# Seven products instead of eight from chunk 4 on in a spectral filter with a gated MLP

## The chip, the cores and the metric

The kernel runs on one core of a Trainium2 chip. The metric is the device time of one execution in microseconds (us); the time before is the median of three runs. A separate execution was taken with the hardware profiler; all lines of the profile come from it. Its engines are named PE (TensorE, matmuls), PEld (TensorE's weight loads, which overlap PE), DVE (VectorE), ACT (ScalarE), POOL (GpSimd) and SP (SyncE, whose queue issues all transfers).

## What is computed

Two branches on the same x of 8192 tokens by 448 features, joined at the end. Cut to what matters:

```
xn = layernorm(x)                                  # over the 448 features
s  = irfft2( mlp( rfft2(xn) ) )                    # per frequency: 4 blocks of 112 features,
                                                   # complex 112x112, relu, 112x112, soft shrink
g  = silu( (gelu(x @ w_gate) * (x @ w_up)) @ w_down )   # 448 -> 1792 -> 448
out = x + s * g
```

In the kernel both branches start from the same x in float32. A float32 value is carried as two float16 values, a high and a low part, and a float32 product as three float16 matmuls (high by high, high by low, low by high) accumulated in one PSUM bank.

## The kernel before

**Two streams of work share the engines.** The foreground is the gated MLP (function `ffn`, line 1895, which runs `chunk`, line 1945). The 8192 tokens are 16 chunks of 512; the 1792 inner features are 14 tiles of 128. Pass 0 takes tiles 0 to 7 for chunks 2 to 15 (chunks 0 and 1 are done at the start in another way, `plain`), pass 1 takes tiles 8 to 13 for all 16. The partial result of pass 0 goes to memory (`prt`) and is added in pass 1. The background is the spectral branch in three phases: phase 1 (`chunk1`, line 837) normalises 16 chunks of x, prepares their token factors (`xts` in memory) for the MLP and does the first step of the transform; phase 2 (`group`, line 2268) does the frequencies; phase 3 (`tiles3`, line 2432) does the last step, multiplies by g and stores. Beside phase 1, `weights` (line 2774) prepares the weight tiles.

**Units and the down projection of a chunk.** In both products the 2x2 block product is done with seven instead of eight block products (Strassen-Winograd). In the gate and up projections, `unit` (line 1433) does this throughout: a pair of tiles is a unit of 7 products of 10 or 12 matmuls of 256 columns, four units a chunk in pass 0. In the down projection there are two forms. `down` (line 1866) is the plain one: for each of 4 blocks of 128 tokens and each tile, three matmuls of 448 columns into a bank bd. `down2` (line 1682) does seven products of 224 columns: it needs factors of w_down (sums of its blocks, prepared by `factors2` and stored in memory as `dsp`) and sums of h, the MLP's inner result. The sums are made by `sums` (line 1535) inside each unit, from the tiles gl and u, by additions, casts and subtractions; they are stored in the tiles h and left. The tile gl has one buffer in pass 0; it is taken by the second gelu of a unit and given back when `sums` has read it. The partial results of `down2` meet in four tiles th, first written by ACT, later added to by DVE.

**When the seven products begin.** At the start of a chunk, `chunk` looks at two flags (line 1948). `products` is set by `weights` once the first four factor tiles are stored, plus 3 us (line 2795). If it is set, and the pass is 1 or the chunk's number is at least 9, the flag `seven` is set for good, and `factors_in(0)` (line 1236) is issued 2 us later: 26 transfers from `dsp` into the tiles dw, wt and left, where dw until then held the plain w_down.

**The order of the work.** All instructions are put in order by a planner at build time (`Pace`, line 59). It keeps a modelled time, the modelled end of each engine's work and a modelled cost of each operation; each engine then runs its instructions in the order in which the planner emitted them. Foreground work is emitted when its inputs are due; background work waits until the engine is modelled as free (`clear`, line 99). The table STEPS (line 43) is read by modelled time, and each row holds, after its time: us added to the landing of a transfer; how far an engine may be booked ahead before background waits; a factor on modelled durations of ACT, DVE and POOL; a shift in the choice between DVE and POOL where either can do an operation (`Either`, line 295); and a factor on the spacing of background work. The background's spacing is T1 and DT for phase 1 (line 886: chunk c starts at T1, then each DT later times that factor), END2 for phase 2 and END3 for phase 3 (line 2388: the pieces left are spread over the time left).

Of the kernel before, what the change touches and what calls it, by code (L numbers as in the profile page):

```python
# [22 lines left out]
NG = 16  # L23
# [35 lines left out]
class Pace:  # L59
# [498 lines left out]
def afno_geglu_kernel(ctx, tc, x, gu, raw, wd, mlp, b1, b2, c_m, c_mt, c_small, c_rows, out):  # L558
# [103 lines left out]
    def ev(*key):  # L662
        return EV.setdefault(key, Event())
# [742 lines left out]
    state = {"direct": NG}  # L1406
# [538 lines left out]
    def chunk(p, i):  # L1945
        nf = PF[p][1]
        nxt = (p, i + 1) if i + 1 < NG else ((1, 0) if p == 0 else None)
        if "products" in state and "seven" not in state and (p or i >= 9):
            state["seven"] = True
            pace.spawn(later(lambda: factors_in(0)), pace.now + 2.0)  # L1950
        seven = "seven" in state
        if "h" not in state:
            state["h"] = yield from HT.get()
        h = state["h"]

        def hv(f, s):
# [72 lines left out]
        yield from down(p, i, 1, 0, cut, hv)  # L2029
        yield pe()  # L2030
        for a in (0, 1):
            yield from down(p, i, a, cut, nf, hv)
            yield pe()
        for a in (2, 3):
            yield from down(p, i, a, 0, nf, hv)
            yield pe()
        HT.put(state.pop("h"))

    def later(fn):
        fn()  # L2040
        return
        yield
# [809 lines left out]
```

## Time and profile before

| What | us |
|---|---|
| time before, median of 3 runs | 1727.75 (1726.9 to 1728.06) |
| the profiled execution's own time | 1729.31 |
| its span (first to last instruction) | 1727.2 |
| chunk 2 of pass 0 begins | 142 |
| chunk 4 of pass 0 begins | 259 |
| chunk 9 of pass 0 begins, the first with seven products | 538 |
| last transfer of phase 1's token factors issued | 635 |
| first load of phase 3 issued | 1472 |
| last matmul ends | 1721 |

The times of chunks are the starts of their first matmul of the kind bx<-xta,wt. In the profile, an operation is named out<-in by the program's tiles without buffer numbers, and nearly all of them carry line 290, where the planner records them; so groups are told apart by their tiles and shapes. bx and by are the PSUM banks of the units, bd those shared by the down projection and the background. In a row of the stages, each engine has its busy time and, in brackets, the number of its instructions; then follow the clock granted to TensorE (1.00 is full), the mean busy share of the 16 DMA engines, and GB/s. In a row of the timeline, the start comes first, then how long the run of like instructions lasted to its modelled end, and their number at the end.

### The profile page before, as it was taken

To read this page: it belongs to the slowest core of one execution; us is meant where nothing else is said; L and a number is where in the kernel's file an instruction comes from. 1 tells how busy PE (TensorE), PEld (TensorE's weight loads), DVE (VectorE), ACT (ScalarE), POOL (GpSimd) and SP (SyncE) were. 2 spreads that over 40 slices of the span, in tenths; PEclk is the share of its full clock that TensorE was granted. 3 is DMA by queue.
4 is the path that set the end of the run, shared out by engine and by line. 5 is a ranking of instruction groups with operands and counts; after the bars stand their busy time and mean duration, and the time that the engine had idled before them with its cause. 6 is when DMAs were issued, how large, how long until landed. Compare 5 with 4: busy or idle time off the path is not lost.

```text
span 1727.2 us, 41012 instructions
## 1 busy us (share of the span) xinstructions
PE 1709.1 (99%) x15654; PEld 1435.5 (83%) x15654; DVE 1345.0 (78%) x2317; ACT 1103.3 (64%) x2242; POOL 1014.2 (59%) x1410
## 2 busy tenths in 40 slices
PE   9999999999999999999999999999999999999998
PEld 4447677766777999998999999999999999889886
DVE  8998888778777878778786777787776786577776
ACT  6767766676756657678676667777676665333333
POOL 2487656677735785456374466654555654555556
PEclk9999999999999999999999999999999999999999
DMA  7348986997756753253535875454645544999996
GB/s 275 119 154 256 276 237 207 265 281 202 231 163 189 208 135 77 60 128 88 131 91 172 214 174 122 123 135 109 156 123 137 120 105 123 280 321 314 296 306 229
DMA packets 438308, 316.62 MB, mean 183 GB/s; under 512 B 305792, under 2 KB 409600, under 8 KB 436320
## 3 DMA queue, kind: packets, MB, share of 16 engines
q1 hardware_dynamic: 437824, 313.99, 64.4%
q8 instruction: 122, 2.00, 0.5%
q14 instruction: 74, 0.61, 0.1%
q10 hardware_dynamic: 288, 0.03, 0.0%
HBM read 137.93 MB, written 108.25 MB: 143 GB/s over the span
## 4 chain that ended last, share of the span: by engine, by line
PE 87%; DVE 6%; ACT 2%; DMA 2%; POOL 2%; issue 1%; SPq 0%; POOLq 0%; DVEq 0%; ACTq 0%
PE bd L290 35%; PE bx L290 30%; PE by L290 22%; DMA prt<-th 1%; DVE st L290 1%; ACT wt L290 1%; DVE raws L290 0%; POOL st L290 0%; DVE ysb L290 0%; DVE wt L290 0%; DVE dw L290 0%; DVE left L290 0%; DVE u L290 0%; DMA xta<-xts 0%; DVE h L290 0%
## 5 line engine op out<-in xcount | busy, mean ns | idle before, releaser
L290 PEld LDWEIGHTS <-wt 128*128 128x128 f16 x9142 | 885.4, 98 | 160.2 <-issue 8.2
L290 PE MATMUL bx<-xta,wt 128*128 128x256 f16 (+1 forms) x2819 | 354.0, 275 | 3.5 <-ACT by L290 2.6
L290 PEld LDWEIGHTS <-h 128*128 128x128 f16 x2711 | 259.8, 98 | 75.5 <-POOL h L290 1.6
L290 PE MATMUL by<-xtb,wt 128*128 128x256 f16 x2080 | 255.2, 273 | 0.4 <-DVE by L290 0.3
L290 PE MATMUL bd<-dw,h 128*128 128x448 f16 (+1 forms) x1536 | 243.1, 306 | 1.0 <-DVE ysb L290 0.7
L290 POOL TENSOR_TENSOR wt<-wt 128x256 f32<-128x256 f32 x181 | 140.2, 775 | 94.0 <-DVE wt L290 84.7
L290 PE MATMUL bx<-xtb,wt 128*128 128x256 f16 x1248 | 154.3, 274 | 2.2 <-DVE v L290 2.2
L290 PE MATMUL by<-xta,wt 128*128 128x256 f16 (+1 forms) x899 | 123.8, 282 | 0.1
L290 POOL TENSOR_TENSOR h<-wt,h 128x512 f16<-128x512 f32 (+1 forms) x92 | 96.1, 1058 | 35.9 <-ACT h L290 35.4
L290 DVE TENSOR_TENSOR by<-bx,u 128x512 f32<-128x512 f32 x104 | 72.4, 696 | 52.9 <-PE bx L290 44.9
L290 ACT ACTIVATE u<-by,fc 128x512 f32<-128x512 f32 (+1 forms) x118 | 73.6, 636 | 51.5 <-PE by L290 49.4
L290 PE MATMUL bx<-left,wt 128*128 128x256 f16 x816 | 99.9, 272 | 0.0
L290 DVE TENSOR_TENSOR v<-bx,u 128x512 f32<-128x512 f32 x104 | 71.4, 686 | 36.1 <-PE bx L290 35.5
L290 PE MATMUL bd<-dw,wt 128*128 128x224 f16 (+1 forms) x816 | 97.6, 264 | 0.5 <-DVE left L290 0.5
L290 POOL CAST zs<-t 112x256 f16<-112x256 f32 (+2 forms) x45 | 21.3, 474 | 123.1 <-DVE t L290 107.9
L290 ACT COPY u<-by 128x512 f32<-128x512 f32 x104 | 60.8, 585 | 50.2 <-PE by L290 49.4
L290 ACT CAST h<-wt 128x512 f16<-128x512 f32 (+1 forms) x128 | 68.5, 536 | 31.4 <-DVE wt L290 25.1
L290 PE MATMUL bd<-w2t,wn 113*128 113x112 f16 (+1 forms) x1152 | 77.6, 212 | 0.0
L290 ACT COPY by<-bx 128x512 f32<-128x512 f32 x104 | 59.8, 575 | 21.1 <-PE bx L290 20.8
L290 PE MATMUL bd<-wt,h 128*128 128x224 f16 x603 | 72.0, 259 | 0.8 <-POOL h L290 0.8
L290 PEld LDWEIGHTS <-wn 113*128 113x128 f16 (+1 forms) x1152 | 69.1, 97 | 2.1
L290 DVE SCALAR_TENSOR_TENSOR u<-by,fc,u 128x512 f32<-128x512 f32 (+1 forms) x86 | 55.2, 656 | 18.7 <-PE by L290 12.9
(283 smaller groups left out, 3764.8 us busy)
## 6 DMA issues: line engine op xcount, KB each, us to landing
xts<-sx SPq DMA_DIRECT2D x32, 480.0 KB, 3.6
x<-in_x SPq DMA_DIRECT2D x17, 896.0 KB, 6.2
t<-ysb SPq DMA_DIRECT2D x64, 224.0 KB, 3.8
prt<-th SPq DMA_DIRECT2D x64, 224.0 KB, 3.2
vt<-va SPq DMA_DIRECT2D x256, 56.0 KB, 2.1
left<-prt SPq DMA_DIRECT2D x64, 224.0 KB, 3.7
u<-t SPq DMA_DIRECT2D x32, 448.0 KB, 6.0
x<-in_x SPq DMA_DIRECT2D x32, 448.0 KB, 6.6
```

What stands on the lines that cost most here:

```text
L290: return self.pace.issue(self.name, kind, out, ins, lambda: fn(out, *args, **kw))
```

## The change

Four edits. The first lets the seven products begin at chunk 4 instead of chunk 9 of pass 0. The second sets the first phase's chunks at another start and spacing. The third moves the due time of phase 3, END3. The fourth replaces the table STEPS from end to end; four of its rows are shown. Nothing else of the program differs.

```diff
-STEPS = ((0, 2.75, 0.05, 1.0, 0.0, 1.0), (15, 2.75, 0.05, 1.0, 0.0, 1.0),
+STEPS = ((0, 2.75, 0.05, 1.0, -0.3, 1.0), (15, 2.75, 0.05, 1.0, -0.3, 1.0),
...
-(125, 2.5, 0.15, 1.04, 0.0, 1.0), (150, 2.5, 0.15, 1.04, 0.0, 1.0),
+(125, 2.0, 0.05, 1.07, 0.2, 1.0), (150, 2.0, 0.05, 1.07, 0.2, 1.0),
...
-(375, 3.0, 0.05, 1.03, -0.2, 0.9), (400, 3.0, 0.05, 1.03, -0.2, 0.9),
+(375, 2.0, 0.05, 1.08, 0.0, 1.06), (400, 2.0, 0.05, 1.08, 0.0, 1.06),
...
-(1525, 1.25, 0.05, 1.025, -0.5, 1.0), (1550, 1.25, 0.05, 1.025, -0.5, 1.0),
+(1525, 2.0, 0.05, 0.965, -0.5, 1.16), (1550, 2.0, 0.05, 0.965, -0.5, 1.16),
...
-    T1, DT = 84.0, 34.0
+    T1, DT = 80.0, 32.5
...
-        if "products" in state and "seven" not in state and (p or i >= 9):
+        if "products" in state and "seven" not in state and (p or i >= 4):
...
-    END1, END2, END3 = T1 + NG * DT + 12.0, 1450.0, 1716.0
+    END1, END2, END3 = T1 + NG * DT + 12.0, 1450.0, 1704.0
```

END1 is used nowhere else.

More of the change, by code (lines that the diff above doesn't have):

```diff
@@ L42 @@
 EPS = 1e-5
-STEPS = ((0, 2.75, 0.05, 1.0, 0.0, 1.0), (15, 2.75, 0.05, 1.0, 0.0, 1.0), (25, 2.75, 0.05, 0.96, 0.2, 1.0), (35, 2.75, 0.05, 0.96, 0.2, 1.0), (45, 2.75, 0.05, 1.08, 0.1, 1.0), (55, 2.75, 0.05, 1.08, 0.1, 1.0), (65, 2.75, 0.05, 1.07, 0.0, 1.0), (75, 2.75, 0.05, 1.07, 0.0, 1.0), (87, 2.75, 0.15, 0.98, -0.1, 1.0), (100, 2.75, 0.15, 0.98, -0.1, 1.0), (125, 2.5, 0.15, 1.04, 0.0, 1.0), (150, 2.5, 0.15, 1.04, 0.0, 1.0), (175, 2.5, 0.15, 1.04, 0.2, 1.0), (200, 2.5, 0.15, 1.04, 0.2, 1.0), (225, 3.0, 0.15, 1.08, -0.2, 1.0), (250, 3.0, 0.15, 1.08, -0.2, 1.0), (275, 3.0, 0.15, 1.08, -0.2, 1.0), (300, 3.0, 0.15, 1.08, -0.2, 1.0), (325, 3.0, 0.05, 1.03, -0.2, 1.0), (350, 3.0, 0.05, 1.03, -0.2, 1.0), (375, 3.0, 0.05, 1.03, -0.2, 0.9), (400, 3.0, 0.05, 1.03, -0.2, 0.9), (425, 2.5, 0.15, 1.04, -0.5, 1.06), (450, 2.5, 0.15, 1.04, -0.5, 1.06), (475, 2.5, 0.1, 1.04, 0.0, 1.0), (500, 2.5, 0.1, 1.04, 0.0, 1.0), (525, 2.5, 0.1, 1.04, -0.3, 1.0), (550, 2.5, 0.1, 1.04, -0.3, 1.0), (575, 2.5, 0.1, 1.04, -0.2, 0.94), (600, 2.5, 0.1, 1.04, -0.2, 0.94), (625, 2.5, 0.1, 1.06, -0.2, 0.94), (650, 2.5, 0.1, 1.06, -0.2, 0.94), (675, 2.5, 0.1, 1.03, -0.2, 0.94), (700, 2.5, 0.1, 1.03, -0.2, 0.94), (725, 2.5, 0.1, 1.03, -0.3, 0.94), (750, 2.5, 0.1, 1.03, -0.3, 0.94), (775, 3.0, 0.05, 1.04, -0.5, 1.0), (800, 3.0, 0.05, 1.04, -0.5, 1.0), (825, 2.5, 0.05, 1.02, -0.5, 1.0), (850, 2.5, 0.05, 1.02, -0.5, 1.0), (875, 2.5, 0.05, 1.05, -0.5, 1.0), (900, 2.5, 0.05, 1.05, -0.5, 1.0), (925, 2.5, 0.05, 1.05, -0.5, 0.94), (950, 2.5, 0.05, 1.05, -0.5, 0.94), (975, 2.5, 0.05, 1.05, -0.5, 0.94), (1000, 2.5, 0.05, 1.05, -0.5, 0.94), (1025, 4.0, 0.05, 1.05, -0.5, 0.9), (1050, 4.0, 0.05, 1.05, -0.5, 0.9), (1075, 4.0, 0.05, 1.05, -0.5, 0.75), (1100, 4.0, 0.05, 1.05, -0.5, 0.75), (1125, 2.75, 0.05, 1.04, 0.0, 0.94), (1150, 2.75, 0.05, 1.04, 0.0, 0.94), (1175, 1.75, 0.05, 1.075, 0.0, 1.0), (1200, 1.75, 0.05, 1.075, 0.0, 1.0), (1225, 1.75, 0.05, 1.045, -0.5, 0.94), (1250, 1.75, 0.05, 1.045, -0.5, 0.94), (1275, 1.75, 0.05, 1.055, -0.5, 1.0), (1300, 1.75, 0.05, 1.055, -0.5, 1.0), (1325, 1.25, 0.05, 0.995, -0.5, 1.03), (1350, 1.25, 0.05, 0.995, -0.5, 1.03), (1375, 1.25, 0.05, 0.995, -0.5, 0.93), (1400, 1.25, 0.05, 0.995, -0.5, 0.93), (1425, 1.25, 0.05, 0.995, -0.5, 0.93), (1450, 1.25, 0.05, 0.995, -0.5, 0.93), (1475, 1.25, 0.05, 1.025, -0.5, 1.0), (1500, 1.25, 0.05, 1.025, -0.5, 1.0), (1525, 1.25, 0.05, 1.025, -0.5, 1.0), (1550, 1.25, 0.05, 1.025, -0.5, 1.0), (1575, 1.25, 0.05, 1.055, -0.5, 1.06), (1600, 1.25, 0.05, 1.055, -0.5, 1.06), (1625, 1.25, 0.05, 1.055, -0.5, 1.06), (1650, 1.25, 0.05, 1.055, -0.5, 1.06), (1675, 1.25, 0.1, 1.045, -0.5, 1.06), (1700, 1.25, 0.1, 1.045, -0.5, 1.06), (1725, 2.75, 0.05, 0.94, 0.4, 1.0))
@@ new lines @@
+STEPS = ((0, 2.75, 0.05, 1.0, -0.3, 1.0), (15, 2.75, 0.05, 1.0, -0.3, 1.0), (25, 2.75, 0.05, 0.96, 0.2, 1.0), (35, 2.75, 0.05, 0.96, 0.2, 1.0), (45, 2.75, 0.05, 1.08, 0.3, 1.0), (55, 2.75, 0.05, 1.08, 0.3, 1.0), (65, 2.75, 0.05, 1.07, 0.0, 1.0), (75, 2.75, 0.05, 1.07, 0.0, 1.0), (87, 2.75, 0.05, 1.07, 0.0, 1.0), (100, 2.75, 0.05, 1.07, 0.0, 1.0), (125, 2.0, 0.05, 1.07, 0.2, 1.0), (150, 2.0, 0.05, 1.07, 0.2, 1.0), (175, 2.0, 0.2, 1.07, 0.2, 1.0), (200, 2.0, 0.2, 1.07, 0.2, 1.0), (225, 2.0, 0.05, 1.08, 0.2, 1.06), (250, 2.0, 0.05, 1.08, 0.2, 1.06), (275, 2.0, 0.05, 1.08, -0.1, 1.06), (300, 2.0, 0.05, 1.08, -0.1, 1.06), (325, 2.0, 0.05, 1.08, -0.1, 1.06), (350, 2.0, 0.05, 1.08, -0.1, 1.06), (375, 2.0, 0.05, 1.08, 0.0, 1.06), (400, 2.0, 0.05, 1.08, 0.0, 1.06), (425, 3.0, 0.3, 1.03, -0.2, 0.9), (450, 3.0, 0.3, 1.03, -0.2, 0.9), (475, 2.5, 0.3, 1.04, 0.0, 1.0), (500, 2.5, 0.3, 1.04, 0.0, 1.0), (525, 2.5, 0.3, 1.04, 0.2, 1.0), (550, 2.5, 0.3, 1.04, 0.2, 1.0), (575, 2.5, 0.05, 1.04, 0.0, 1.0), (600, 2.5, 0.05, 1.04, 0.0, 1.0), (625, 2.5, 0.3, 1.04, -0.3, 0.9), (650, 2.5, 0.3, 1.04, -0.3, 0.9), (675, 2.5, 0.05, 1.04, -0.3, 0.9), (700, 2.5, 0.05, 1.04, -0.3, 0.9), (725, 2.5, 0.1, 1.03, -0.4, 1.0), (750, 2.5, 0.1, 1.03, -0.4, 1.0), (775, 3.0, 0.05, 1.08, -0.4, 1.0), (800, 3.0, 0.05, 1.08, -0.4, 1.0), (825, 2.5, 0.05, 1.0, -0.5, 1.0), (850, 2.5, 0.05, 1.0, -0.5, 1.0), (875, 2.5, 0.05, 1.0, -0.5, 1.0), (900, 2.5, 0.05, 1.0, -0.5, 1.0), (925, 2.5, 0.05, 1.05, -0.5, 0.94), (950, 2.5, 0.05, 1.05, -0.5, 0.94), (975, 2.5, 0.05, 1.02, -0.5, 0.94), (1000, 2.5, 0.05, 1.02, -0.5, 0.94), (1025, 3.25, 0.05, 1.02, -0.2, 0.94), (1050, 3.25, 0.05, 1.02, -0.2, 0.94), (1075, 3.25, 0.05, 1.02, -0.5, 0.94), (1100, 3.25, 0.05, 1.02, -0.5, 0.94), (1125, 3.25, 0.05, 1.02, -0.5, 0.94), (1150, 3.25, 0.05, 1.02, -0.5, 0.94), (1175, 3.5, 0.05, 1.02, -0.5, 0.84), (1200, 3.5, 0.05, 1.02, -0.5, 0.84), (1225, 1.75, 0.05, 1.045, -0.5, 0.94), (1250, 1.75, 0.05, 1.045, -0.5, 0.94), (1275, 1.75, 0.05, 1.045, -0.5, 0.94), (1300, 1.75, 0.05, 1.045, -0.5, 0.94), (1325, 2.25, 0.05, 1.045, -0.5, 0.94), (1350, 2.25, 0.05, 1.045, -0.5, 0.94), (1375, 2.25, 0.05, 1.045, -0.5, 0.94), (1400, 2.25, 0.05, 1.045, -0.5, 0.94), (1425, 1.25, 0.05, 0.965, -0.5, 1.0), (1450, 1.25, 0.05, 0.965, -0.5, 1.0), (1475, 1.25, 0.05, 0.965, -0.5, 1.1), (1500, 1.25, 0.05, 0.965, -0.5, 1.1), (1525, 2.0, 0.05, 0.965, -0.5, 1.16), (1550, 2.0, 0.05, 0.965, -0.5, 1.16), (1575, 2.0, 0.05, 0.965, -0.5, 1.16), (1600, 2.0, 0.05, 0.965, -0.5, 1.16), (1625, 2.0, 0.05, 0.965, -0.5, 1.16), (1650, 2.0, 0.05, 0.965, -0.5, 1.16), (1675, 1.25, 0.05, 1.055, -0.4, 1.06), (1700, 1.25, 0.05, 1.055, -0.4, 1.06), (1725, 2.75, 0.05, 0.94, 0.4, 1.0))
```

## Prediction

> **What bounds the kernel now.** I read the page first: busy time by engine and the chain that ended last.
>
> ```profile
> span 1727.2 us, 41012 instructions
> PE 1709.1 (99%) x15654; PEld 1435.5 (83%) x15654; DVE 1345.0 (78%) x2317; ACT 1103.3 (64%) x2242; POOL 1014.2 (59%) x1410
> PE 87%; DVE 6%; ACT 2%; DMA 2%; POOL 2%; issue 1%; SPq 0%; POOLq 0%; DVEq 0%; ACTq 0%
> ```
>
> PE is busy 99% of the span and is 87% of the chain. A busy PE need not be a PE at its rate, so next come the stages (PE's busy time is the second figure), and what PE waited for from 140 to 540 us (us in total, times, longest).
>
> ```profile
> core 0: us, PE busy (x) PEld busy (x) DVE busy (x) ACT busy (x) POOL busy (x), PEclk, DMA share, GB/s
> 150.00:200.00 50.00, 47.40 (x343) 34.01 (x341) 40.88 (x81) 34.85 (x74) 31.30 (x59) 0.97 0.86 244
> 250.00:540.00 290.00, 287.71 (x2169) 211.46 (x2168) 228.55 (x429) 191.88 (x370) 191.26 (x343) 1.00 0.77 224
> 540.00:1000.00 460.00, 458.94 (x4780) 423.90 (x4778) 352.75 (x610) 316.38 (x683) 267.50 (x362) 1.00 0.52 134
> 1000.00:1700.00 700.00, 699.51 (x7032) 638.11 (x7030) 525.19 (x828) 410.50 (x817) 389.40 (x445) 1.00 0.67 186
> ...
> PE bx L290 <- ACT by L290: 2.6, 2, 1.9
> PE bx L290 <- DVE v L290: 1.4, 1, 1.4
> PE bd L290 <- DVE ysb L290: 0.7, 1, 0.7
> PE by L290 <- DVE by L290: 0.3, 1, 0.3
> ```
>
> From 250 us on PE is idle for 2.3 + 1.1 + 0.5 us in 1450. So whatever leaves PE's stream of matmuls leaves the time, as long as the other engines keep up, and whatever they add to PE's waits comes back whole.
>
> **The change, part by part.** *Fewer columns.* In each of chunks 4 to 8 of pass 0 the plain down projection (4 token blocks x 8 row tiles x 3 matmuls of 448 columns = 96) gives way to seven products (7 x 4 pairs x 2 halves x 3 = 168 of 224 columns, and one of 64). Prices come from the start of one run to the start of the next:
>
> ```profile
> 191.92 10.96 PE L290 MATMUL bd<-dw,h 128*128 128x448 f16 x57
> 202.71 0.49 PE L290 MATMUL bx<-xta,wt 128*128 128x256 f16 x3
> ...
> 641.32 1.31 PE L290 MATMUL bd<-dw,h 128*128 128x224 f16 x12
> 642.47 0.74 PE L290 MATMUL bd<-wt,h 128*128 128x224 f16 x6
> ```
>
> The wide one costs (202.71 - 191.92) / 57 = 189.3 ns, the narrow one 1.15 / 12 = 95.8 ns. A chunk's down projection goes from 96 x 189.3 = 18.17 us to 168 x 95.8 = 16.09, and by the same scale 0.03 for the 64 columns: 2.05 us less. Five chunks: **10.2 us off PE**.
>
> *Does it start at chunk 4?* The flag needs the last store of the first four factor tiles (and 3 us); chunk 4 begins with its first product:
>
> ```profile
> 225.87 0.55 SPq L290 DMA_DIRECT2D dsp<-wo  x1
> ...
> 259.07 1.15 PE L290 MATMUL bx<-xta,wt 128*128 128x256 f16 x9
> ```
>
> That leaves some 30 us. These tiles are background work; the new table books DVE, ACT and POOL work 3% longer there (1.07 for 1.04) and the chunks of the first phase come 4% closer, which is a few us of the 30.
>
> *The factors' loads move.* They are 26 issues on SP's queue, which took
>
> ```profile
> 541.98 1.26 SPq L290 DMA_DIRECT2D dw<-dsp  x2
> 543.30 12.75 SPq L290 DMA_DIRECT2D wt<-dsp  x16
> 556.09 3.75 SPq L290 DMA_DIRECT2D left<-dsp  x8
> ```
>
> 17.9 us in one piece, and now stand at about 262 us instead. They wait for the last plain matmul of chunk 3, which is over by then. Behind them wait the first phase's stores of transposed tokens, its loads of x and the weight tiles. The nearest deadline among those, for the chunk that was being stored at 310 us:
>
> ```profile
> 310.77 1.96 SPq L290 DMA_DIRECT2D xts<-sx  x3
> ...
> 406.34 4.63 SPq L290 DMA_TRANSPOSE xta<-xts  x1
> ```
>
> It is stored about 92 us before it is read back, so 18 us more on SP costs PE nothing: I take zero; if that cover were gone, 18 us once.
>
> *More vector work.* Seven products need sums of h. Chunk 7 (plain) against chunk 9 (seven products, the first phase still running), first in all, then for the tile gl, the tile left in chunk 9, and the partial results th:
>
> ```profile
> 427.90:484.10 56.20, 56.08 (x426) 41.53 (x425) 40.67 (x70) 38.45 (x75) 39.51 (x68) 1.00 0.84 242
> 314.80:370.60 55.80, 55.80 (x425) 41.43 (x424) 46.87 (x83) 40.23 (x79) 43.36 (x71) 1.00 0.89 264
> 538.10:594.20 56.10, 56.10 (x528) 51.08 (x526) 40.85 (x68) 37.14 (x77) 37.08 (x63) 1.00 0.79 216
> ...
> 427.90:484.10 56.20, 0.00 (x0) 0.00 (x0) 4.21 (x5) 5.37 (x9) 5.63 (x4) 1.00 0.84 242
> 538.10:594.20 56.10, 0.00 (x0) 0.00 (x0) 9.96 (x17) 7.32 (x17) 8.79 (x12) 1.00 0.79 216
> 538.10:594.20 56.10, 8.60 (x83) 6.84 (x72) 3.41 (x5) 3.95 (x8) 2.86 (x3) 1.00 0.79 216
> 538.10:594.20 56.10, 2.05 (x3) 2.40 (x4) 0.00 (x0) 1.00 0.79 216
> ...
> L290 POOL TENSOR_TENSOR u<-u 128x256 f32<-128x256 f32 x4 | 3.4, 846 | 1.8 <-DVE u L290 1.6
> ```
>
> DVE gains 5.75 + 3.41 + 2.05 = 11.2 us a chunk, POOL 3.16 + 2.86 + 3.4 = 9.4: 20.6 us at most (operations between gl and left count twice), some 6 on ACT, which has 15 idle. Chunk 5, the fullest (second row), has 8.9 us idle on DVE and 12.4 on POOL: 21.3. It just fits, and chunk 9 ran PE without a gap (56.10 of 56.10). What does not fit is background (statistics, token factors, far weight tiles), which the planner puts off and which has the 92 us above. I cost it at zero. Its cover is thin, though; the rivals price that.
>
> *Spacing, table, due time.* They issue nothing new. T1 and DT bring the first phase's chunks 4 to 26 us forward before the table's factors, the table shifts what is booked when, END3 packs phase 3 12 us tighter. They act on PE through its waits alone. Below: the waits listed above for 140 to 540 us (chunks 2 to 8) are 5.0 us, and the longest also cost clock:
>
> ```profile
> 155.35 1.25 PE L290 MATMUL bx<-xta,wt 128*128 128x256 f16 x10 [1.89 <-ACT by L290]
> ...
> 153.70:160.00 6.30, 4.65 (x28) 3.44 (x28) 6.20 (x14) 4.33 (x10) 5.52 (x13) 0.75 0.94 260
> ```
>
> At a mean clock of 0.75 over 6.3 us, 1.6 us went. All gone would be 6.6 us less. Above: as many new ones. I take no net change, as the row nearest to the new state (chunk 9) has none and chunks 2 and 3 stay as they are. The Trainium skill (TensorE: Matmul & The Clock Gate, "Why this matters for your kernels") asks for idle gaps under about 3 us to keep the clock; by it the 1.9 us wait would have cost itself alone, and a new one of that size 1.9 us where this trace says 3.5. The trace does not agree with it here, and I price by the trace.
>
> **Sum.** Span 1727.2 - 10.2 = 1717.0. The median of the runs shown stands 0.55 above the span of the profiled execution (whose own time, 1729.31, is 2.1 above it). So 1727.75 - 10.2 = **1717.5 us**.
>
> **The rivals.** *(B) It starts a chunk late.* If the fourth factor tile slips 30 us, chunk 5 is the first: 4 x 2.05 = 8.2, 1719.5. Against it: the margin above.
>
> *(C) A wait in each chunk.* There is one gl buffer, held until the sums are done. In chunk 10:
>
> ```profile
> 610.06 0.69 ACT L290 ACTIVATE gl<-bx,fc 128x512 f32<-128x512 f32 x1
> 617.37 0.89 DVE L290 TENSOR_TENSOR left<-gl,left 128x256 f16<-128x256 f32 x1
> 618.44 0.69 ACT L290 ACTIVATE gl<-bx,fc 128x512 f32<-128x512 f32 x1 [0.86 <-PE bx L290]
> 611.99 2.78 PE L290 MATMUL bx<-xta,wt 128*128 128x256 f16 x24
> ```
>
> It was held from 610.06 to 618.26, 0.2 us before the next unit wanted it; and PE took that bank of bx again 1.2 us after the first gelu ended (610.75 to 611.99). With some 1.4 us more on the chain, which far-weight work could add, PE waits once a chunk. At 1.4 us, like the wait on v above, that is 7.2 - 2.3 (what chunks 4 to 8 lose now) = 4.9 back: 1722.4.
>
> *(D) Slower: DVE becomes the bound in chunks 4 to 8.* It is busy 44 us a chunk now (228.55 x 55.8 / 290), and a chunk will last 53.75. It has room for 9.7 us of the new 20.6; with 11.8 the 2.05 us are lost again, and that is the point from which it decides. If it draws 14.5 and nothing can be put off, 5 x 4.8 = 24 come back and 10.2 go: 1741. For it: chunk 9 gave DVE 11.2. Against it: the first phase and the weight tiles, which DVE also serves there, can be put off, and the choice between DVE and POOL goes by whichever is free.
>
> *(E) A matmul costs by its number, not its columns.* 73 more at 95.8 ns would be 7.0 us a chunk, 35 in all: 1763. The two runs above speak plainly against it (189.3 to 95.8 for 448 to 224 columns). The Trainium skill (same page, "Back-to-back issue gap") states about 81 ns for 128 columns and 131 for 512 in a stream of paired weight loads and matmuls; on a line between, 448 would be 123 ns and 224 would be 93, and the change would add some 20 us, an estimate from that page. The trace does not agree.
>
> *(F) The transfers bound phase 3.* From its first load to the old due time:
>
> ```profile
> 1472.00:1716.00 244.00, 242.76 (x2219) 214.63 (x2217) 179.69 (x246) 94.44 (x165) 140.94 (x146) 1.00 0.95 300
> 1500.00:1550.00 50.00, 50.00 (x464) 44.71 (x463) 37.23 (x53) 18.05 (x32) 23.55 (x24) 1.00 1.05 323
> ```
>
> 244 x 0.95 = 232 us of transfers, and 232 us are left. If 1.00 is the most, this fits with nothing over, and uneven demand could cost 5 us: 1722.5. Against it: 1.05 and 323 GB/s were reached with PE at 50.00 of 50.
>
> **How the numbers follow.** Forecast 63%, B 6%, C 19%, D 7%, F 4%, E 1%. A measurement of this kernel tells about 0.2%, 3.5 us. Faster by more: 63 + 6 + 16 of C + 3 of F = 88%. Within: 3 of C, 1 of F, 2 of D = 6%. Slower: 5 of D, 1 of E = 6%. The range runs from 1713.0 (4.5 of the 6.6 us of old waits and clock gone) to 1723.5 (C with one wait more); it leaves out D, E and the far parts of C.
>
> **What would show it.** Matmuls of 448 columns into bd from dw and h fall from 768 to 288, those of 224 columns rise by 840; the loads of the factors stand near 262 us. Chunks 4 to 8 each end about 2 us earlier, adding up to 10 by the end of chunk 8, and the lead stays 10 us to the end. B: 384 of 448 columns remain. C: PE waits on DVE v or ACT by, one a chunk, between 260 and 530 us. D: DVE without gaps there. F: PE waits after 1470 us on th or left. The prediction is wrong if the lead at 540 us isn't near 10 us, or shrinks after it.

## The result and the profile after

| Kernel | us, median | runs | ratio to before, with its 95% interval |
|---|---|---|---|
| before | 1727.75 | 5 (1726.90 to 1728.87) | 1 |
| changed | 1735.68 | 5 (1733.54 to 1737.79) | 1.0047 (1.0034 to 1.0061) |

The change makes the kernel slower by 7.9 us; 1717.5 us had been forecast. First the page of the changed kernel (its profiled execution took 1737.79 us), then its matmuls into bd from dw and h by shape (times, busy us, mean ns, idle before them):

```profile
span 1736.0 us, 41908 instructions
PE 1703.6 (98%) x16019; PEld 1469.6 (85%) x16019; DVE 1402.7 (81%) x2425; ACT 1122.6 (65%) x2309; POOL 1046.3 (60%) x1450
PE 86%; DVE 6%; POOL 3%; DMA 1%; ACT 1%; issue 1%; SPq 0%; DVEq 0%; ACTq 0%; POOLq 0%
```

```profile
L290 PE MATMUL bd<-dw,h 128*128 128x224 f16 x978 | 114.3, 259 | 1.5 <-ACT th L290 1.2 <-POOL h L290 0.4
L290 PE MATMUL bd<-dw,h 128*128 128x448 f16 x288 | 57.1, 353 | 0.0
```

The wide matmuls fell from 768 to 288, and all matmuls rose by 16019 - 15654 = 365 = 840 + 5 - 480. So the edit does what it says, from chunk 4 on. PE is busy 5.5 us less, and yet the span is 8.8 us longer: the gain went into waits. The stages of the changed kernel, in the columns of the prediction's rows, and what PE waited for in them; the waits after 540 us of before come last, for comparison:

```profile
250.00:540.00 290.00, 285.42 (x2590) 251.62 (x2589) 243.38 (x442) 193.47 (x397) 223.25 (x352) 0.99 0.75 212
540.00:1000.00 460.00, 452.46 (x4635) 414.18 (x4634) 371.91 (x672) 321.12 (x689) 278.27 (x395) 1.00 0.54 139
1000.00:1700.00 700.00, 697.16 (x7049) 635.10 (x7047) 541.49 (x857) 417.70 (x840) 375.25 (x433) 1.00 0.67 186
```

From 250 to 540 us, changed kernel, in full:

```profile
PE bx L290 <- DMA xta<-xts: 2.0, 1, 2.0
PE bx L290 <- ACT by L290: 1.4, 2, 1.0
PE bd L290 <- ACT th L290: 1.2, 1, 1.2
```

From 540 to 1470 us, changed kernel (the four largest of ten rows):

```profile
PE bx L290 <- ACT gl L290: 2.0, 1, 2.0
PE bd L290 <- DVE zs L290: 1.9, 2, 1.2
PE bx L290 <- DVE v L290: 1.9, 3, 0.8
PE bd L290 <- DVE bd L290: 1.2, 2, 1.0
```

The same stretch of before, in full:

```profile
PE bx L290 <- DVE v L290: 0.7, 1, 0.7
PE bd L290 <- DVE left L290: 0.5, 1, 0.5
PE bd L290 <- DVE zs L290: 0.3, 1, 0.3
```

From 540 to 1000 us PE is idle 7.5 us where before it was idle 1.1, on foreground work that the change leaves as it was, for many tiles, never longer than 2.0 us. From 250 to 540 us a transfer heads the list for which before PE never waited there. Ahead of the early products, at the start of chunk 2, PE also waits 2.9 us for a transfer of this kind.

To follow such small waits through many kernels I use one number, the **loss**: over all matmuls, the time from the start of one to the start of the next, less the columns of the first at 2400 per us and 2.5 ns (which gives the prediction's 189.3 and 95.8 ns for 448 and 224 columns). It holds waits and time at a lower clock. PE's work by this measure is 1692.0 us before and 1681.9 changed, 10.1 less. Losses in us, by the stage in which they stand:

| Kernel | 0-250 | 250-540 | 540-700 | 700-1475 | later | sum |
|---|---|---|---|---|---|---|
| before | 17.0 | 3.9 | 1.2 | 3.0 | 1.8 | 26.9 |
| changed | 20.5 | 7.9 | 6.2 | 10.3 | 1.8 | 46.6 |

19.7 us more of losses against 10.1 us less of work, less 0.8 us behind the last matmul: that is the 8.8 us of the span. 3.5 of them stand ahead of the first chunk that the early products touch, 4.0 in the chunks that they touch, 12.3 behind (all rounded).

### The profile page after: what moved, and what is told of

It is laid out like the page before. It is cut to its first block, busy times and chain, and to the rows that moved or that the text cites. A ratio compares the mean times of both kernels' runs of the same rounds, so it can differ in the third digit from the quotient of the medians.

```text
span 1736.0 us, 41908 instructions
## 1 busy us (share of the span) xinstructions
PE 1703.6 (98%) x16019; PEld 1469.6 (85%) x16019; DVE 1402.7 (81%) x2425; ACT 1122.6 (65%) x2309; POOL 1046.3 (60%) x1450
## 4 chain that ended last, share of the span: by engine, by line
PE 86%; DVE 6%; POOL 3%; DMA 1%; ACT 1%; issue 1%; SPq 0%; DVEq 0%; ACTq 0%; POOLq 0%
PE bd L290 35%; PE bx L290 29%; PE by L290 22%; POOL h L290 1%; POOL sx L290 1%; POOL wt L290 1%; DVE h L290 1%; DVE wt L290 1%; DVE u L290 1%; DVE left L290 0%; DMA xta<-xts 0%; DVE wn L290 0%; DVE st L290 0%; SPq L290 0%; DMA x<-in_x 0%
## 5 line engine op out<-in xcount | busy, mean ns | idle before, releaser
L290 PEld LDWEIGHTS <-wt 128*128 128x128 f16 x9142 | 886.4, 98 | 172.4 <-issue 18.6
L290 POOL TENSOR_TENSOR wt<-wt 128x256 f32<-128x256 f32 x185 | 146.1, 790 | 83.3 <-DVE wt L290 73.5
L290 PE MATMUL bd<-dw,h 128*128 128x224 f16 (+1 forms) x1266 | 171.4, 280 | 1.5 <-ACT th L290 1.2
L290 POOL TENSOR_TENSOR h<-wt,h 128x256 f16<-128x256 f32 (+1 forms) x89 | 93.0, 1056 | 48.5 <-ACT h L290 48.4
L290 ACT COPY u<-by 128x512 f32<-128x512 f32 x104 | 60.8, 585 | 46.1 <-PE by L290 44.6
L290 DVE TENSOR_TENSOR v<-bx,u 128x512 f32<-128x512 f32 x104 | 71.2, 685 | 20.3 <-PE bx L290 19.6
L290 PE MATMUL bd<-wt,h 128*128 128x224 f16 x693 | 84.3, 259 | 1.2 <-DVE h L290 0.6
L290 PEld LDWEIGHTS <-left 128*128 128x128 f16 x864 | 81.8, 98 | 2.4 <-issue 1.0
```

The lines of the kernel that those rows point to most:

```text
L290: return self.pace.issue(self.name, kind, out, ins, lambda: fn(out, *args, **kw))
```

## The experiments

All ratios are to runs of before beside them (medians 1727.65 to 1728.42). Three theories. **L, load**: the sums for the early products load DVE, POOL and ACT while the first phase runs, and PE waits for them, or for the first phase that they delay. **T, table**: the new table or spacing places work badly. **R, rerolled order**: the old table holds rows that were picked for exactly the old order of instructions; any other order, whatever its cause, brings back waits that these rows avoid.

### One part alone

The first puts only the seven products at chunk 4, the second only the new table, the third leaves out the table alone, the fourth has only the spacing and due time.

```diff
# seven products alone (e1_seven)
-(p or i >= 9)
+(p or i >= 4)
# new table alone (e2_table): the STEPS line of the change
# all but the table (e3_old_table): the change with the old STEPS line
# spacing alone (e4_spacing)
-    T1, DT = 84.0, 34.0
+    T1, DT = 80.0, 32.5
...
-END1, END2, END3 = T1 + NG * DT + 12.0, 1450.0, 1716.0
+END1, END2, END3 = T1 + NG * DT + 12.0, 1450.0, 1704.0
```

> The kernel before with the seven products from chunk 4 on, and nothing else: old table, old spacing, old due time. PE's matmuls fall by 10.2 us as in the changed kernel. Theory L (the five chunks' sums of h load DVE and POOL, the first phase slips, phase 2 is squeezed and PE waits): waits as in the changed kernel, about 20 us more than before, so 1734 to 1738 us, and phase 1's last token factors at about 690 us instead of 635. Theory T (the new table misplaces work): the old table keeps its few waits, 1717 to 1721 us, phase 1 ending near 640. Theory R (any other order of the instructions brings waits back that the old table was picked to avoid for one order): 10 to 20 us of new waits spread over the span, 1727 to 1738 us, whatever phase 1 does.

> The kernel before with the new table alone; the seven products begin at chunk 9 as before, so PE has all its old matmuls. L: the loads of chunks 4 to 8 are the old ones, so 1727 to 1731 us. T: the 20 us of waits of the changed kernel stay and its 10.2 us gain goes: 1744 to 1750 us. R: 10 to 20 us of new waits, 1738 to 1748 us.

> The changed kernel with the old table: seven products from chunk 4, new spacing, new due time. L: 1734 to 1738 us, as the changed kernel. T: 1717 to 1721 us. R: 1727 to 1738 us, and not the same waits as in the run with the seven products alone, since the order differs again.

> The kernel before with the new spacing of phase 1 (80.0, 32.5) and the new due time (1704), old table, seven products from chunk 9. L and T: little, 1726 to 1731 us (denser background before 600 us, more idle after). R: an order that the old table was not picked for, 1735 to 1748 us with 8 to 20 us of new waits spread over the span.

| Kernel | us | ratio | 0-250 | 250-540 | 540-700 | 700-1475 | later | sum |
|---|---|---|---|---|---|---|---|---|
| seven alone | 1749.67 | 1.0123 (1.0106 to 1.0140) | 15.7 | 11.9 | 14.0 | 14.8 | 3.0 | 59.3 |
| table alone | 1761.66 | 1.0197 (1.0182 to 1.0212) | 19.9 | 10.1 | 3.1 | 17.5 | 9.6 | 60.3 |
| all but the table | 1759.30 | 1.0180 (1.0165 to 1.0196) | 19.1 | 20.1 | 5.6 | 16.3 | 6.4 | 67.4 |
| spacing alone | 1756.10 | 1.0158 (1.0140 to 1.0177) | 18.7 | 3.9 | 13.0 | 8.2 | 9.5 | 53.3 |

Each part alone costs 22 to 34 us, and all together 8. So the parts don't add up: the new table is worth 23.6 us to the rest of the change (1759.30 to 1735.68), and costs 34 without it. All four came out slower than any of the three theories had it, so the sizes of all three were wrong. By direction alone R fits all four: L had the table and the spacing nearly free, T had the two with the old table and the early products faster. L has two marks: the two with seven products from chunk 4 have the highest losses between 250 and 540 us, and their first phase ends late, as L had it (last store of token factors at 703 and 713 us, in the other two at 631 and 618).

### The order moved by a hair

If R holds, a step that changes nothing but the planner's order must cost as much. T1 goes up by 0.3 us, or END2 by 1 us, in both kernels.

```diff
# before, T1 (j1_before_t1)
-    T1, DT = 84.0, 34.0
+    T1, DT = 84.3, 34.0
# changed, T1 (j2_after_t1)
-    T1, DT = 80.0, 32.5
+    T1, DT = 80.3, 32.5
# before and changed, END2 (j3_before_end2, j4_after_end2)
-    END1, END2, END3 = T1 + NG * DT + 12.0, 1450.0, ...
+    END1, END2, END3 = T1 + NG * DT + 12.0, 1451.0, ...
```

> The kernel before with phase 1 starting 0.3 us later (84.3 for 84.0) and nothing else: the same operations, no more load at any place, the same table. Theory R (another order loses what the table was picked for): 15 to 30 us of waits of PE come back, 1742 to 1758 us. Theories L and T (the load of the early sums; bad entries of the new table): neither is in this kernel, so 1726 to 1730 us.

> The changed kernel with phase 1 starting 0.3 us later (80.3 for 80.0). R: the new table was picked for the changed kernel's own order and loses its worth with it, 1745 to 1760 us. L and T: load and table are the same, so 1733 to 1738 us.

> The kernel before with the due time of phase 2 at 1451 instead of 1450, which moves the spacing of its 64 pieces by a sixty-fourth of a us. Until 640 us every instruction stands where it stood. R: no new wait before 640 us and 5 to 15 us after it, 1732 to 1743 us. L and T: 1726 to 1730 us.

> The changed kernel with the same edit, phase 2 due at 1451. Until its phase 2 begins at about 700 us nothing moves. R: the waits up to 700 us stay (about 21 us between 100 and 700), those after rise by 3 to 12 us, 1738 to 1748 us. L and T: 1733 to 1738 us.

| Kernel | us | ratio | 0-250 | 250-540 | 540-700 | 700-1475 | later | sum |
|---|---|---|---|---|---|---|---|---|
| before, T1 84.3 | 1755.47 | 1.0152 (1.0137 to 1.0167) | 16.4 | 10.2 | 11.5 | 11.6 | 4.3 | 54.1 |
| changed, T1 80.3 | 1736.80 | 1.0046 (1.0031 to 1.0061) | 19.1 | 5.3 | 7.2 | 10.4 | 1.8 | 43.8 |
| before, END2 1451 | 1744.26 | 1.0089 (1.0072 to 1.0106) | 18.2 | 4.7 | 1.2 | 9.3 | 7.7 | 41.1 |
| changed, END2 1451 | 1737.98 | 1.0055 (1.0040 to 1.0071) | 20.6 | 6.0 | 7.2 | 10.0 | 2.4 | 46.1 |

**R is shown for before**: 0.3 us in one start time costs 28 us, as much as the parts of the change (22 to 34). 1 us in END2, which moves the order only from about 840 us on, costs 16.5, just over R's 1743. There the losses of before nearly stay until 700 us and rise by 12.2 from there on, and 5.1 more lie behind the last matmul (the profiled execution took 1748.29, 4.0 above the median, so a part is its own). What is shown is that the neighbours of before have waits that before lacks; that its rows were picked for this is the likely reason, which no run shows. Order means the whole plan here. The planner also chooses between DVE and POOL, and with T1 at 84.3 DVE got 23 operations more than before and POOL 30 fewer; no run parts the sequence from that choice. The page with T1 at 84.3:

```profile
PE 1715.9 (98%) x15654; PEld 1436.8 (82%) x15654; DVE 1361.0 (78%) x2340; ACT 1102.6 (63%) x2249; POOL 996.8 (57%) x1380
```

The changed kernel doesn't answer alike. Its T1 step left the order of every engine as it was, so it is the changed kernel once more and tests nothing. Its END2 step changed the order from about 980 us on, and the two intervals (1.0040 to 1.0071 and 1.0034 to 1.0061) overlap. By this one step it stands in no such hollow there, and has less to lose.

### Pairs without a table of their own

To see what the seven products are worth where the table favours neither side: the changed kernel without them and without the spacing, the partner of the T1 step, and a joined table.

```diff
# changed, but seven at 9 (k2_no_seven)
-(p or i >= 4)
+(p or i >= 9)
# changed, but old T1, DT and END3 (k1_no_spacing)
# before, T1 84.3, seven at 4 (k3_seven_t1)
# before, seven at 4, old rows of STEPS below 225, new ones from there (k4_late_table)
```

> The changed kernel with the seven products at chunk 9 again; its spacing, due time and table stay. PE's work goes back up by 10.2 us. If the load of the early sums is what costs the waits (L), they fall: the losses of 250 to 540 us, 7.9 with the change, go to about 4, the first phase ends near 640 us instead of 691, and the time is within some 5 us of the changed kernel's 1735.7. If a table fits only the order that it was picked for (R), this is one more order without a table: losses between 41 and 67 us in all as in the single edits, 1742 to 1768, wherever in the span they fall.

> The changed kernel with the old spacing of the first phase and the old due time of phase 3; seven products from chunk 4 and the new table stay. If the spacing is needed to make room for the early sums (L), losses rise between 250 and 700 us, by 8 or more over the changed kernel's 14.1, and not elsewhere. If a table fits only its own order (R), losses rise anywhere: 41 to 67 us in all, 1731 to 1757. If the new table is simply better for seven products (T), about the changed kernel's 1735.7.

> The kernel before with T1 84.3 and the seven products from chunk 4: the partner of the run that moved T1 alone (1755.47, losses 54.1 us, of these 10.2 between 250 and 540 us). Both orders have no table of their own, so the difference shows what the seven products are worth where the table favours neither. R: about 10 us less, 1745, give or take the 12 us by which such orders differ among themselves. L: the 10 us come back as waits between 250 and 540 us, losses there 18 or more, about 1755.

> Seven products from chunk 4, old spacing and due time, and a table joined from both: the old rows up to 225 us, the new ones from there. Until about 225 us the order is that of the run with the seven products alone, whose losses up to 250 us were 15.7 us (20.5 with the whole change). If the rows from 225 us on serve seven products as such (T), the rest keeps the 26 us of the changed kernel, 42 in all, about 1731. If they serve only their own order (R), the rest draws 30 to 50 us: 1735 to 1755. L: losses of 250 to 540 us at 8 or more.

| Kernel | us | ratio | 0-250 | 250-540 | 540-700 | 700-1475 | later | sum |
|---|---|---|---|---|---|---|---|---|
| changed, seven at 9 | 1752.52 | 1.0142 (1.0127 to 1.0157) | 19.9 | 13.7 | 3.6 | 10.5 | 4.2 | 52.0 |
| changed, old spacing | 1759.36 | 1.0185 (1.0168 to 1.0202) | 19.6 | 12.6 | 8.3 | 17.3 | 10.3 | 68.0 |
| T1 84.3, seven at 4 | 1754.58 | 1.0155 (1.0140 to 1.0171) | 15.6 | 18.0 | 10.4 | 12.1 | 6.3 | 62.3 |
| joined table | 1759.33 | 1.0183 (1.0168 to 1.0198) | 14.8 | 14.3 | 15.4 | 21.7 | 2.6 | 68.8 |

Without the early products the changed kernel comes out as R had it (1742 to 1768), and not within 5 us of 1735.7, as L had it. Its first phase ends at 624 us again, as L had it, but its losses between 250 and 540 us rose to 13.7, where L had 4. The joined table missed T's 1731 by 28 us and lies above R's range too, and so does the old spacing (1759.36 for 1757 at most). The pair at T1 84.3 gave 0.9 us for the seven products, as L had it. Now there are four orders with a table of another and seven at 9 (table alone, spacing alone, T1 84.3, changed with seven at 9), and five with seven at 4 (seven alone, all but the table, old spacing, T1 84.3 with seven, joined). Their means are 1756.4 us each: losses 54.9 and 65.2. **Without a table of their own the early seven products win nothing that these runs can show: 10.1 us off PE, 10.3 us more of losses**, 8.9 of these between 250 and 700 us (17.3 to 26.1). The sums of single kernels spread by some 4 us about these means, so the difference of the means is good to about 6. (The END2 steps keep the order of their kernel for half the span, and are left out.) The waits say the same. Between 250 and 540 us PE waits 4.0 to 7.6 us in each of the five for the tile left, which the sums write, and in the changed kernel, which needs it as often, never. In the joined table:

```profile
PE bd L290 <- DVE left L290: 4.9, 3, 1.7
PE bd L290 <- ACT left L290: 2.7, 3, 1.3
```

Both R (28 us between before and its neighbours) and L (these 10) are at work; the next runs take the order out.

### The order kept

In these kernels the planner is charged as before, and only what an instruction does is changed, so all engines run the same list (with repeats in the kernels that do an operation three times). The narrower kernels leave out a part of the output columns, the thin ones most of each sum. The first two edits are alone and together in the first three kernels.

```diff
# narrower (f1_narrow, f3_both): plain down projection, real width of the matmul
+k = 394 if p == 0 and 4 <= i <= 8 and not first else D
...
+nc.tensor.matmul(ps[:, 0:k], l, r[:, 0:k], start=first, stop=last)
# three times (f2_repeat, f3_both): the low part of h in glu
+pace.times = 3 if p == 0 and 4 <= state["chunk"][1] <= 8 else 1
 B.tensor_sub(h[:, f0:f0 + 2, 1, cs], v, h[:, f0:f0 + 2, 0, cs])
# thin (f4_thin: in the changed kernel; f5_thin_old: in all but the table): inside sums
+pace.thin = 16 if p == 0 and 5 <= i <= 8 else 0
...
+fn(out[..., 0:k], *(a[..., 0:k] for a in args), **kw)
# narrower late (g1_narrow_late): in prod2 of before
+c_ = 180 if p == 1 and 3 <= i <= 7 and (j or n) else DH
```

> The kernel before with every engine's order of instructions kept. In the plain down projections of chunks 4 to 8, 92 of 96 matmuls are 394 columns wide instead of 448 (their outputs lack the rest): 92 x 54 columns = 2.07 us a chunk, 10.35 us in all, as much as the change takes off PE. If what leaves PE's stream leaves the time (the prediction's first step), 1717.4. If an order is fitted to PE's pace too, so that the waits come back where PE arrives earlier at the same other work, between 1720 and 1727.

> The kernel before with its order kept; in chunks 4 to 8 each subtraction that makes the low part of h is carried out three times instead of once (the same result each time): 16 more operations of 128x512 a chunk, half on DVE and half on POOL, at some 0.7 and 1.1 us about 5.5 us on DVE and 9 on POOL a chunk, about what the sums add to POOL and half of what they add to DVE. If vector work at run time is what PE waits for (L), some 5 to 15 us of new waits between 260 and 640 us, 1732 to 1743. If the engines have room and only the order counts (R), less than 2 us, 1729.

> Both edits of the last two kernels at once, the order of before kept: PE's stream 10.35 us shorter and 16 vector operations a chunk more. If the order is what costs in the change (R), about 1718. If vector work takes PE's gain back (L), 1727 or more. The prediction's own sum for this state (PE less, vector work hidden) is 1717.4.

> The kernel before with every engine's order kept. In five chunks of pass 1 (1159 to 1375 us, the second phase beside them) 560 of the 224-column matmuls of the seven products are 180 columns wide (their outputs lack the rest): 560 x 44 columns = 10.27 us off PE, as much as the narrowing in chunks 4 to 8, which gave 0.6. If any order holds PE to the pace it was made for, again less than 2 us: 1726 to 1728. If it is the fuller engines between 250 and 540 us (DVE busy 79%, POOL 66%, ACT 66% there, in 1000 to 1700 us 75%, 56% and 59%), more comes through here: 5 to 10 us, 1718 to 1723.

> The changed kernel with every engine's order kept; in chunks 5 to 8 the operations of the sums work on 16 columns instead of 256 or 512 (the products then take wrong numbers). That frees some 7 us on DVE and as much on POOL and 5 on ACT a chunk at run time. If the sums' load is what PE waits for (L), the losses of 250 to 700 us, 14.1 with the change, fall to about the 5.1 of before: about 1727. If the order holds PE up (R), they stay: 1733 to 1736.

> The change with the old table (1759.3, losses of 250 to 700 us 25.7), every engine's order kept; in chunks 5 to 8 the sums work on 16 columns instead of 256 or 512 (the products then take wrong numbers). With the new table the same took 5.1 us of losses there and 4.0 of the time. If the load of the sums is what PE waits for in an order without its table (L), 10 us or more of the losses go there, 1749 or less. If the order holds PE up (R), 5 or less, 1754 to 1759.

| Kernel | us | ratio | 0-250 | 250-540 | 540-700 | 700-1475 | later | sum |
|---|---|---|---|---|---|---|---|---|
| narrower, chunks 4-8 | 1727.78 | 0.9994 (0.9985 to 1.0003) | 14.8 | 15.3 | 1.2 | 2.8 | 1.8 | 35.9 |
| three times | 1786.38 | 1.0334 (1.0320 to 1.0348) | 15.9 | 53.8 | 11.9 | 3.9 | 1.8 | 87.5 |
| both | 1783.70 | 1.0320 (1.0306 to 1.0334) | 19.8 | 58.3 | 11.7 | 3.9 | 1.8 | 95.6 |
| narrower late | 1720.52 | 0.9955 (0.9941 to 0.9968) | 16.6 | 3.9 | 1.2 | 5.1 | 1.8 | 28.6 |
| changed, thin sums | 1731.69 | 1.0020 (1.0011 to 1.0028) | 19.0 | 3.2 | 5.8 | 10.3 | 1.8 | 40.1 |
| all but table, thin sums | 1749.08 | 1.0119 (1.0106 to 1.0133) | 18.4 | 7.5 | 6.9 | 16.2 | 6.4 | 55.4 |

Single profiled executions scatter. Until 250 us the first four kernels and the END2 step of before run what before runs, and their first column goes from 14.8 to 19.8, for 17.0; the order of the changed kernel, run once more as T1 80.3, loses 43.8 us in all for 46.6.

**Narrower.** 10.3 us off PE in chunks 4 to 8 are worth nothing that can be measured; the losses of that stage rise by 11.4. The waits from 250 to 540 us show how:

```profile
PE bx L290 <- ACT by L290: 6.6, 3, 2.8
PE bx L290 <- DVE v L290: 1.4, 1, 1.4
PE by L290 <- DVE by L290: 1.4, 1, 1.4
PE bd L290 <- DVE xs L290: 0.7, 2, 0.4
```

One of the three on ACT is at the start of chunk 5. ACT's timeline there, first in before, then in the narrower kernel, whose first line is PE's (start, length, what):

```profile
312.72 0.76 ACT L290 ACTIVATE x<-x,st 128x448 f32<-128x448 f32 x1
...
315.20 0.63 ACT L290 ACTIVATE th<-bd,ms 128x448 f32<-128x448 f32 x1
315.73 0.75 ACT L290 ACTIVATE x<-x,st 128x448 f32<-128x448 f32 x1
316.38 0.19 ACT L290 ACTIVATION_READ_ACCUMULATOR x<-x,st 128x1 f32 x1
316.47 0.58 ACT L290 COPY by<-bx 128x512 f32<-128x512 f32 x1
```

```profile
310.48 1.47 PE L290 MATMUL bx<-xta,wt 128*128 128x256 f16 x12
310.58 0.76 ACT L290 ACTIVATE x<-x,st 128x448 f32<-128x448 f32 x1
...
313.18 0.63 ACT L290 ACTIVATE th<-bd,ms 128x448 f32<-128x448 f32 x1
313.71 0.75 ACT L290 ACTIVATE x<-x,st 128x448 f32<-128x448 f32 x1
314.36 0.19 ACT L290 ACTIVATION_READ_ACCUMULATOR x<-x,st 128x1 f32 x1
314.45 0.58 ACT L290 COPY by<-bx 128x512 f32<-128x512 f32 x1
```

PE begins chunk 5 4.3 us earlier than before (310.48 against the 314.8 of the prediction's row). Of these, 2.2 are this execution's own: it began chunk 4 at 256.86 for 259.07, before anything is narrower. The other 2.1 are the narrower matmuls. ACT has the same list in front of the copy that PE needs: three passes over x for the first phase, a cast (in the part left out), and the copy out of the last down projection. It runs them without a pause, but only 2.0 us earlier (314.45 against 316.47), which is no more than the 2.2 it had from the start. The rest is PE's wait, 2.0 us in brackets in its next row, and that is what chunk 4 had gained:

```profile
315.08 1.14 PE L290 MATMUL bx<-xta,wt 128*128 128x256 f16 x9 [2.04 <-ACT by L290]
```

In before the copy was ready just in time: the order was right for PE's old pace, and PE 2 us earlier is PE too early.

**Narrower late.** The same amount off PE in the second phase gave 7.7 us. Both places, before, read as a PE that is hardly ever idle (2.3 us of 290, and 0 of 216). The row from 1159 to 1375 us of before, and then of the narrower kernel, which is idle 1.4 us there:

```profile
1159.00:1375.00 216.00, 216.00 (x2267) 199.97 (x2265) 164.44 (x275) 151.63 (x308) 117.32 (x136) 1.00 0.54 132
```

```profile
1159.00:1375.00 216.00, 214.60 (x2349) 197.03 (x2347) 166.42 (x286) 155.28 (x318) 121.17 (x142) 1.00 0.56 136
```

The shares of DVE (76% there, 79% between 250 and 540 us) hardly tell the two apart; POOL's (54% and 66%) and the transfers' (0.54 and 0.77) do a little. The experiment does.

**Three times.** 80 operations more in five chunks cost 3.3%, 58 us. From 250 to 540 us:

```profile
250.00:540.00 290.00, 253.04 (x1794) 177.99 (x1792) 217.13 (x354) 159.46 (x312) 216.97 (x333) 0.94 0.71 201
```

DVE is busy 217 of 290 us, less than the 228.55 of before (the stretch now holds less of the work), and yet PE is idle 37 us. The idle time of DVE and POOL is no room that work can be put into where it comes up; with PE's work cut too (both), 1783.70. So neither R's 1729 nor its 1718 was right, and L's 1732 to 1743 for the repeats alone was far too low.

**Thin sums.** Taking most of the sums' run time out of chunks 5 to 8 gives 10.2 us in the order without its table, where L had 10 or more, and 4.0 in the changed kernel, where 1731.69 lies between L's 1727 and R's 1733 (the intervals of the changed kernel with and without thin sums do not overlap). All but the table, and the same with thin sums, from 250 to 540 us:

```profile
250.00:540.00 290.00, 276.93 (x2479) 241.63 (x2478) 242.16 (x410) 186.71 (x382) 221.57 (x346) 0.98 0.69 199
```

```profile
250.00:540.00 290.00, 284.45 (x2601) 251.63 (x2599) 208.31 (x422) 179.23 (x403) 182.98 (x356) 1.00 0.74 211
```

34 us less on DVE and 39 less on POOL, and 7.5 us less idle on PE. So L is right about size where the order is not picked: the load takes back about what PE gains. With the new table more than half of that is gone, but the losses behind 540 us stay in both kernels with thin sums (17.9 for the changed kernel's 18.3, 29.5 for 28.3 with the old table): they are not made by what the sums of chunks 5 to 8 take at run time.

## Why the prediction was wrong, point by point

**Right.** *Fewer columns*: 10.1 us off PE for 10.2, counted by columns, and from 262 to 522 us the changed kernel's narrow matmuls do follow each other at 96 ns (median). *The start at chunk 4*: yes; rival B fell. *Rival E*: fell by the same 96 ns, and with it the 20 us that the prediction worked out from the Trainium skill (TensorE: Matmul & The Clock Gate, "Back-to-back issue gap"). *The end of phase 3* (F): losses from 1475 us on are 1.8 in both.

**The step that failed**: "I take no net change", for the waits under spacing, table and due time. It took the 5.0 us of waits of before as what the kernel has, and new ones as likely as fewer. But before's losses of 26.9 us belong to one order; four neighbours with other orders and seven at 9 have 52 to 60. A change that moves the order starts from there, and its own table must win it back. The new one does in part: 65.2 us is the mean of orders with early products and another's table, 46.6 what is left. Counted so, the change is -10.1 (PE's work) + 10.3 (losses of the early products in orders that are not picked) + 9.4 (the new table wins 18.6 us where the old one, for its order, wins 28.0) - 0.8 = 8.8, the 8.8 of the span. The 10.3 and the 9.4 add up to the 19.7 of losses that were measured; how they share it is good to some 6 us. Why the new rows win less is open. One reading is that the first phase ends later (the last store below) and squeezes the second. No run singled it out, and the nine kernels above hardly bear it out: in the five with early products the first phase ends at 691 to 713 us, in the four others at 618 to 631, and the losses behind 700 us are 22.2 and 18.9 on average, with a spread of some 4 and 6 us. The last stores of the first phase in before, and then changed:

```profile
634.64 1.54 SPq L290 DMA_DIRECT2D xts<-sx  x2
```

```profile
684.22 4.31 SPq L290 DMA_DIRECT2D xts<-sx  x3
```

**The first step**, too: "whatever leaves PE's stream of matmuls leaves the time, as long as other engines keep up". Its condition does not hold between 250 and 540 us, and idle PE of 2.3 us in 290 did not show it: with the order kept, 0.6 of 10.35 us came through there, and 7.7 of 10.27 in the second phase. The Trainium skill (Perfetto Trace Analysis, "Identifying the Most-Contended Engine") warns that the busy time of matmuls is a poor measure and has TensorE's headroom judged by, among others, the busy share of the weight loads. PEld is busy 73% between 250 and 540 us and 93% between 1159 and 1375; by the Trainium skill the second place is nearer its limit, and these two runs agree, though two places are no proof of it.

**More vector work**, costed at zero because 20.6 us fit into 21.3 idle: mis-sized. By the thin sums it costs 10.2 us with the old table and up to 4.0 with the new one. Rival D had the direction, not the form: DVE is not without gaps (243.38 of 290), and no time of D's came. C named DVE v and ACT by, one wait a chunk from 260 to 530 us. PE waited there twice for ACT by, 1.4 us in all, and not for DVE v; the larger part came later. (One wait of C's more than its 1722.4 makes 1723.8, not the 1723.5 at the end of the range; nothing hangs on it.)

**The factors' loads**, costed at zero, too: the 92 us of cover belonged to another transfer. SP's queue in the changed kernel:

```profile
266.67 1.65 SPq L290 DMA_DIRECT2D dw<-dsp  x2
268.37 14.64 SPq L290 DMA_DIRECT2D wt<-dsp  x16
...
283.05 4.26 SPq L290 DMA_DIRECT2D left<-dsp  x8
...
290.26 5.84 SPq L290 DMA_DIRECT2D xts<-xs  x8
...
300.47 4.84 SPq L290 DMA_TRANSPOSE xta<-xts  x1
305.41 3.53 SPq L290 DMA_TRANSPOSE xtb<-xts  x1
```

The loads hold the queue until 287.3; the stores that piled up follow, and only then the read of chunk 5's tokens, issued 6 us before PE wants it. In before the same read was issued 19 us ahead of the 314.8 at which PE begins that chunk:

```profile
295.91 10.77 SPq L290 DMA_TRANSPOSE xta<-xts  x1
```

PE waits 2.0 us for it until 308.3 (with the clock below, 3.7 of the 7.9 us lost in that stage):

```profile
308.34 0.92 PE L290 MATMUL bx<-xta,wt 128*128 128x256 f16 x4 [1.97 <-DMA xta<-xts]
```

So the nearest deadline behind the loads was this read and not the one that the prediction took. The size differs from one execution to the next: with the same order (T1 80.3) the wait was 0.7 us, and in the other kernels with early products it was 0 to 1.0. In the changed kernel with thin sums PE takes 2.0 us longer over chunk 4, whose work is the same in both, and does not wait, so part of the 4.0 us above is this place and not the sums. No run moved the loads alone.

**The lead.** Chunk 9 begins at 522.61, 15.5 us ahead of before rather than 10; but first-phase matmuls were put off for it (138 of the 174 into bd from xs and m had run by then, in before 162), and by the first load of phase 3 (1472 before) the lead is a lag of 10.5:

```profile
522.61 1.47 PE L290 MATMUL bx<-xta,wt 128*128 128x256 f16 x12
...
1482.55 0.46 SPq L290 DMA_DIRECT2D mt<-c_mt  x1
```

No version that computes all of the output and beats before came out of these runs; by the sum above, one with early products would need rows that win more in its own order.

## What to carry to other kernels

Before a saving on the busiest engine is counted, find out what stands ready just in time beside it: keep the order, make that engine's instructions cheaper in the one stage, and see whether the time follows. A kernel whose schedule was picked for one exact order can stand in a hollow (here 1.5% deep, for 0.3 us in one constant), so an edit is to be compared with neighbours that were picked as little as it, or with a schedule picked for it with as much care. Idle time of the other engines, summed over a chunk, says neither that work fits in nor that PE may come earlier.

## What was not expected of the hardware

A wait of 2.0 us again cost clock, but a longer one did not. The changed kernel around the start of chunk 2, with its wait, and around 306 us:

```profile
145.75 1.47 PE L290 MATMUL bx<-xta,wt 128*128 128x256 f16 x12 [2.89 <-DMA xta<-xts]
143.00:152.00 9.00, 5.60 (x49) 4.72 (x49) 8.87 (x13) 6.89 (x17) 8.04 (x11) 1.00 1.02 244
305.00:312.00 7.00, 5.03 (x34) 3.85 (x32) 3.97 (x9) 1.54 (x4) 2.62 (x3) 0.76 1.09 268
```

At 0.76 for 7 us, 1.7 us went beside the 2.0 of the wait, and a wait of 2.2 us that ended at 160.8 cost as much. The wait of 2.9 us that ended at 145.75 cost nothing beside itself, nor did one of 2.0 us that ended at 602.2: the clock granted behind both is 1.00. So from 1.9 to 2.9 us the length of a wait does not tell here whether it costs clock, and the 3.5 us that the prediction put on a wait of 1.9 us was the price of one case. What decides is open. Where waits come thick it adds up: in the kernel with the operation done three times PE was idle 37 us between 250 and 540 us at a mean granted clock of 0.94, 17 us more, together about the 53.8 of the table. The Trainium skill (TensorE: Matmul & The Clock Gate, "Why this matters for your kernels") names idle gaps above about 3 us as what drops the clock; the waits at 161 and 306 us do not agree with that. The kernel with the operation done three times can't tell, since its waits reach 3.9 us.
